# Half-width weight pieces, and the read-in product M of batch 0 made in two halves

## The chip, the cores and the metric

The kernel runs on one core of a Trainium2 chip. The time is the device time of one execution in microseconds (us). Times given with a profile come from one profiled execution; its span runs from the first to the last instruction of the program.

The engines are TensorE (PE; its weight loads are listed as PEld), VectorE (DVE), ScalarE (ACT), GpSimd (POOL) and SyncE (SP), whose queue issues the transfers (DMA). Each engine works through its own instructions in program order, and waits in that order for what the others deliver.

## The reference, cut to what matters

Attention between 512 tokens and 32 state rows per head goes both ways, and its result runs through an expert block, `w_in`, gelu, `w_out`.

```python
scores = scale * x @ state.T              # B=8, H=8, S=512, Ns=32, D=64
a = softmax(scores);  xread = a @ state
a2 = softmax(scale * state @ x.T);  sread = a2 @ x
y = concat([xread, sread], axis=2)        # (B,H,S+Ns,D) -> (B*(S+Ns), H*D) = (4352, 512)
h = y @ w_in                              # 512 -> 2048
out = (h * sigmoid(1.702 * h)) @ w_out    # 2048 -> 512
```

Both weights come as 64-bit floats and are used as 32-bit ones.

## The kernel before, in words

**The product M.** Since `xread` is `a @ state`, the up product of the token rows is `a @ (state @ w_in)`. For each batch b and each chunk c of 512 columns of `w_in` the kernel makes M(b, c) = state @ w_in[:, c] first, by heads (`att_M`, 16 matmul records of a 64x32 tile by 512 columns through `by_state`, L320, into two PSUM tiles, each copied to SBUF by ACT, L460). The up products then need two contractions over 128 instead of four: `up_x(b, f)` multiplies 128 columns of M by the normalised, transposed weights `aT` of the attention (L524, four records) and ACT applies the gelu (L527). The columns f = 4c to 4c + 3 belong to chunk c. `turn(b, c, then, n)` makes the four up products of a chunk, puts `att_M(*then)` ahead of the last of them, and rounds pieces of weights after the first ones.

**PSUM.** Two pools of two banks each serve this stage: `psA` (`att_ps`: transposes, M, and up products marked spare) and `psH` (up products, warming matmuls, and an M marked spare, such as M(1,0)). A bank is written again only after its last reader is done.

**The weights.** SP loads 64-bit words in 32 pieces of 512 KB (`PIECES`, `load_weight`, L185): 16 of `w_in`, chunk by chunk, each 128 rows by 512 columns, then 16 of `w_out`. Each is turned into 32-bit floats by DVE and ACT: `mask` (DVE, L207), two Relus on ACT for `w_in` (`round_a`, L218 and L219), then `fraction` (L225) and three steps of `round_b` (L236, L239, L243) on DVE. `powers_to(n)` runs the first part for the pieces up to n, `round_to(n)` the second, which also runs the first part three pieces ahead; `rounds(n)` does n more pieces. Program order is written out by hand, so the place of each such call in the list at the end of the kernel (from L1131 on) sets the order on DVE, ACT and SP.

**The start.** Two pieces are loaded, then state and x of batch 0, two more pieces, state and x of batch 1, the rest. `att_xT_arriving` transposes x of batch 0 as it lands and makes its scores in halves; `att_scores` makes the scores of the other direction. DVE subtracts the maxima, ACT takes the exponential (L1146), and `att_x_norm` (L403 to L408) normalises and transposes into `aT`. Batch 1 follows with `att_state`, `att_xT`, `att_scores`, `att_blocks` (L351), `att_x_exp` (L394 to L396) and `att_x_norm`; its `aT` lies in the tile `low`, beside the working rows of the pieces. `keep_warm(n)` fills PE with n matmuls on zeros (L125). M(0,0) is made whole, after piece 3 and after the scores of batch 1; up products 0 to 3 of batch 0 follow, M(1,0), piece 4 and `att_x_norm(1)`, and then turns of four between the two batches. From the first product with `w_out` on (L542, near 78 us), and for the later batches, nothing in the code differs.

Of the kernel before, what the change touches and what calls it, by code (L numbers as in the profile page):

```python
# [10 lines left out]
FP32 = mybir.dt.float32  # L11
I32 = mybir.dt.int32
U32 = mybir.dt.uint32
AF = mybir.ActivationFunctionType
# [6 lines left out]
def kernel(  # L21
# [30 lines left out]
    nc = tc.nc  # L52

    B, H, S, D = x.shape
# [27 lines left out]
    mpool = ctx.enter_context(tc.tile_pool(name="mpool", bufs=1))  # L82
# [4 lines left out]
    psH = ctx.enter_context(tc.tile_pool(name="psH", bufs=2, space=bass.MemoryType.PSUM))  # L87
# [4 lines left out]
    def att_ps(shape, name):  # L92
        return psA.tile(shape, FP32, tag="att", name=name)
# [16 lines left out]
    low = konst.tile([P, 6, S], FP32, name="low")  # L110
# [51 lines left out]
    w_in = [konst.tile([P, NPR, FC], FP32, name=f"w_in_{c}") for c in range(NFC)]  # L162
    w_out = konst.tile([P, NF, DM], FP32, name="w_out")
    w_in_words, w_out_words = moe_w_in.bitcast(I32), moe_w_out.bitcast(I32)

    PIECES = [("i", c, k) for c in range(NFC) for k in range(NPR)] + [("o", f) for f in range(NF)]
    raw, power, begun = {}, {}, {}
    AHEAD = 3

    def load_weight(i):  # L170

        key = PIECES[i]
        nin, room = NFC * NPR, NF // 2
        if i < room or nin - NPR <= i < nin:
            o = 2 * (i % room if i < room else i - (nin - NPR))
            raw[i] = w_out[:, o : o + 2].rearrange("p f n -> p (f n)").bitcast(I32)
        else:
            o = 2 * (i % 4)
            raw[i] = later[:, o : o + 2].rearrange("p f n -> p (f n)").bitcast(I32)
        if key[0] == "i":  # L180
            _, c, k = key
            src = w_in_words[P * k : P * (k + 1), 2 * FC * c : 2 * FC * (c + 1)]
        else:
            src = w_out_words[P * key[1] : P * (key[1] + 1)]
        nc.sync.dma_start(raw[i], src)  # L185

# [6 lines left out]
    for i, v in enumerate((8.0 * most, 8.0 * (most - least))):  # L193
        t = konst.tile([P, 1], FP32, name=f"edge_{i}")
        nc.gpsimd.memset(t, v)
        edge.append(t)

    def words(i):
        w = raw[i].rearrange("p (n w) -> p w n", w=2)
        return w[:, 0].bitcast(U32), w[:, 1]  # L200

    def mask(i):

        _, hi = words(i)
        sc = low[:, 2 + i % (AHEAD + 1)].bitcast(I32)
        power[i] = sc
        nc.vector.tensor_scalar(sc, hi, 0x7FF00000, None, ALU.bitwise_and)  # L207

    def round_a(i):

        if i not in power:
            mask(i)
        sc = power[i]
        if PIECES[i][0] == "o":
            nc.vector.tensor_scalar(sc, sc, most, least, ALU.min, ALU.max)
            nc.vector.tensor_scalar(sc, sc, -least, 8.0, ALU.add, ALU.mult)
            return
        nc.scalar.activation(out=sc.bitcast(FP32), in_=sc, func=AF.Relu, bias=edge[0], scale=-8.0)  # L218
        nc.scalar.activation(out=sc, in_=sc.bitcast(FP32), func=AF.Relu, bias=edge[1], scale=-1.0)  # L219

    def fraction(i):

        key = PIECES[i]
        dst = w_in[key[1]][:, key[2]] if key[0] == "i" else w_out[:, key[1]]
        nc.vector.tensor_scalar(dst.bitcast(I32), words(i)[1], 0xFFFFF, 0x100000, ALU.bitwise_and, ALU.bitwise_or)  # L225
        begun[i] = dst

# [87 lines left out]
    def by_state(b, ps, rhs):  # L315

        for j in range(NPR):
            for g in range(NG):
                rows, st = slice(D * g, D * (g + 1)), slice(Ns * j, Ns * (j + 1))
                nc.tensor.matmul(ps[g][st], A[b]["stT"][rows, st], rhs(rows, j), start=True, stop=True)  # L320
# [77 lines left out]
    def att_x_norm(b):  # L398

        a = A[b]  # L400
        t = a["e1"].rearrange("p g i n -> p (g i) n")
        sm = apool.tile([P, NS1], FP32, tag="sm", name=f"sm_{b}")
        nc.vector.reduce_sum(out=sm, in_=t, axis=AX.X)  # L403
# [4 lines left out]
        nc.vector.transpose(  # L408
            a["aT"].rearrange("p g t -> p (g t)"), a["e1"].rearrange("p g i n -> p (g i n)")
        )  # L410
# [37 lines left out]

    turns = {"M": 0}

    def att_M(b, c, spare=False):

        m = mpool.tile([P, NG, FC], FP32, tag=f"M{turns['M'] % NFC if b < 2 else c}", name=f"M_{b}_{c}")
        turns["M"] += 1
        A[b]["M", c] = m
        name = f"M_{b}_{c}_"
        ps = [psH.tile([P, FC], FP32, tag="h", name=name + str(g)) if spare else att_ps([P, FC], name + str(g)) for g in range(NG)]
        by_state(b, ps, lambda rows, j: w_in[c][rows, j])
        for g in range(NG):
            nc.scalar.copy(m[:, g], ps[g])  # L460


    squares = dram.tile([Ns, NG * NB, NPR, Ns], FP32, name="squares")
# [53 lines left out]

    G = {}

    def up(key, f, ntok, lhs, rhs, spare=False):  # L520
        hps = att_ps([P, ntok], f"h_{key}_{f}") if spare else psH.tile([P, ntok], FP32, tag="h", name=f"h_{key}_{f}")
        n = len(lhs)
        for i in range(n):
            nc.tensor.matmul(hps, lhs[i], rhs[i], start=(i == 0), stop=(i == n - 1))  # L524
        if f % 2 == 0:
            G[key, f // 2] = free.pop(0)
        nc.scalar.activation(out=G[key, f // 2][:, f % 2, :ntok], in_=hps, func=AF.Gelu_apprx_sigmoid)  # L527

    def up_x(b, f, spare=False):
        c, o = divmod(P * f, FC)  # L530
        m = A[b]["M", c]
        up(b, f, S, [m[:, g, o : o + P] for g in range(NG)], [A[b]["aT"][:, g] for g in range(NG)], spare)

    O = {}

# [589 lines left out]
    nper = FC // P  # L1125

    def rounds(n):
        round_to(done["b"] + n)
# [16 lines left out]
    powers_to(3)  # L1145
    nc.scalar.activation(out=A[0]["e1"], in_=A[0]["e1"], func=AF.Exp, scale=scale)  # L1146
    att_scores(0)
    powers_to(2)
    round_to(3, 0)
    powers_to(4)  # L1150
    att_x_norm(0)
    keep_warm(24)
    att_state(1)
    for j in range(NPR):
        keep_warm(2)
        att_xT(1, j)
    att_scores(1)
    keep_warm(3)
    powers_to(4)
    round_to(NPR, 1)  # L1160
    att_M(0, 0)
    powers_to(NPR + 2)


    att_blocks(1)
    att_x_exp(1)
    up_x(0, 0)
    up_x(0, 1)
    up_x(0, 2, True)
    up_x(0, 3, True)  # L1170

# [4 lines left out]
    def turn(b, c, then, n=()):  # L1176

        for i in range(nper):
            if i == nper - 1 and then:
                att_M(*then)  # L1180
            up_x(b, nper * c + i)
            if i < len(n):
                rounds(n[i])

    turn(1, 0, None, [1, 1, 1])
    att_M(0, 1)
    turn(0, 1, (1, 1), [1, 1, 1])
    round_to(3 * NPR)
    turn(1, 1, (0, 2), [1, 1])
    round_to(4 * NPR)  # L1190
# [77 lines left out]
    for b in range(1, B):  # L1268
# [23 lines left out]
        k = 3 if b + 1 < B else 0  # L1292
# [40 lines left out]
```

## Time and profile before

| | |
|---|---|
| median of 8 runs | 713.93 us (713.71 to 714.02) |
| profiled execution | 713.95 us |
| its span | 712.2 us |
| PE busy | 697.9 us |
| DVE busy | 602.1 us |
| ACT busy | 231.3 us |
| pieces of `w_in`: transfers | 16 of 512 KB |
| moved by DMA | 77.10 MB |

The table's busy times are sums over the span. The kernel has stages with different limits, so the views by stage, the timeline and the chain of waits (the work that ended last, followed back) say more than they do. In a timeline line stand the start and the duration in us, the engine, the line of the kernel, the operation, what it writes and reads with shape, how many instructions were merged, and in brackets how long the engine had been idle and what released it. In a line by stage each engine has its busy time and the number of its instructions.

### The profile page before, as it was taken

How to read it: one execution, taken by the hardware profiler on the slowest of the kernel's cores; microseconds unless marked ns; L12 is line 12 of the kernel's file. 1: busy time of each engine (PE TensorE's matmuls, PEld its weight loads, DVE VectorE, ACT ScalarE, POOL GpSimd, SP SyncE). 2: the span in 40 equal slices, each digit the busy share in tenths (PEclk: the TensorE clock that was granted, in tenths of full speed). 3: DMA queues.
4: the chain of work that ended last, by engine and by line, in shares of the span. 5: the costliest groups of instructions: out<-in, count | busy, mean ns of one | idle time of the engine just before them, and what ended most of it. 6: DMA issues, size and time to landing. Idle time of an engine off the chain costs nothing.

```text
span 712.2 us, 12665 instructions
## 1 busy us (share of the span) xinstructions
PE 697.9 (98%) x4975; PEld 557.8 (78%) x4975; DVE 602.1 (85%) x1246; ACT 231.3 (32%) x456; POOL 0.8 (0%) x8
## 2 busy tenths in 40 slices
PE   8989999999999999999999999999999999999996
PEld 3433444457888799888998899879987998899995
DVE  6999899979987999789968997899789997888650
ACT  5686511023214322433233322441343224300210
POOL 0000000000000000000000000000000000000000
PEclk9999999999999999999999999999999999999999
DMA  8921246217743194408550574138431940031001
GB/s 232 365 78 53 93 147 141 117 44 189 188 130 62 34 202 143 88 0 180 164 120 1 112 205 120 29 70 193 140 61 35 201 146 22 0 115 65 16 1 29
DMA packets 143770, 77.10 MB, mean 108 GB/s; under 512 B 113888, under 2 KB 127712, under 8 KB 143712
## 3 DMA queue, kind: packets, MB, share of 16 engines
q1 hardware_dynamic: 143712, 76.31, 41.4%
q8 instruction: 39, 0.64, 0.4%
q14 instruction: 19, 0.16, 0.1%
HBM read 60.29 MB, written 15.99 MB: 107 GB/s over the span
## 4 chain that ended last, share of the span: by engine, by line
PE 93%; ACT 2%; DVE 2%; DMA 2%; SPq 0%; issue 0%; DVEq 0%; ACTq 0%
PE low L696 21%; PE o L1058 17%; PE o L745 14%; PE o L696 10%; PE o L542 8%; PE h L524 7%; PE upx L1058 6%; PE M L320 4%; PE o L585 2%; PE o L320 1%; PE sr L500 1%; PE warm L125 1%; PE upx_sr L1058 1%; DMA out_dram<-osb_sr 1%; DMA xn<-in_x_dram 1%; DVE g L752 1%
## 5 line engine op out<-in xcount | busy, mean ns | idle before, releaser
L1068 DVE TENSOR_TENSOR g<-o,g 128x512 f32<-128x512 f32 (+1 forms) x140 | 88.0, 650 | 51.1 <-PE o L1058 50.1
L745 PE MATMUL o<-w_out,g 128*128 128x256 f32 x448 | 100.5, 380 | 0.0
L745 PEld LDWEIGHTS o<-w_out,g 128*128 128x128 f32 x448 | 84.2, 190 | 16.9 <-issue 5.5
L1065 ACT ACTIVATE g<-g 128x512 f32<-128x512 f32 (+1 forms) x84 | 49.8, 600 | 100.9 <-DVE g L1068 100.9
L1058 PE MATMUL upx<-aT,M 128*128 128x256 f32 x192 | 49.3, 379 | 0.0
L1058 PE MATMUL o<-ta,M 128*128 128x256 f32 x192 | 49.3, 379 | 0.0
L1058 PE MATMUL o<-ta,ms 128*128 128x256 f32 x192 | 48.3, 379 | 0.0
L696 PE MATMUL low<-low,g 128*128 128x128 f32 x336 | 44.4, 275 | 0.0
L460 ACT COPY M<-M 128x512 f32<-128x512 f32 x64 | 33.2, 596 | 28.1 <-PE M L320 28.1
L696 PEld LDWEIGHTS low<-low,g 128*128 128x128 f32 x336 | 40.9, 192 | 0.0
L1058 PEld LDWEIGHTS o<-ta,ms 128*128 128x128 f32 x192 | 36.5, 190 | 5.0
L1058 PEld LDWEIGHTS o<-ta,M 128*128 128x128 f32 x192 | 36.5, 190 | 5.0
L1058 PEld LDWEIGHTS upx<-aT,M 128*128 128x128 f32 x192 | 36.0, 190 | 4.6
L696 PE MATMUL low<-sums,later 128*128 128x128 f32 x280 | 37.1, 275 | 0.0
L696 PEld LDWEIGHTS low<-sums,later 128*128 128x128 f32 x280 | 34.6, 192 | 0.6 <-ACT pu L705 0.2
L320 PE MATMUL M<-w_in,stT 64*32 64x512 f32 x512 | 32.7, 594 | 0.2 <-ACT eT L490 0.2
L524 PE MATMUL h<-low,M 128*128 128x512 f32 x64 | 29.7, 600 | 1.5 <-DVE low L408 1.5
L696 PE MATMUL low<-w_out,g 128*128 128x128 f32 x224 | 29.7, 275 | 0.9 <-DVE pu L701 0.9
L524 PE MATMUL h<-aT,M 128*128 128x512 f32 x64 | 28.7, 599 | 1.4 <-ACT M L460 1.4
L542 PE MATMUL o<-w_out,g 128*128 128x512 f32 x64 | 28.7, 594 | 0.0
L542 PE MATMUL o<-w_out,sums 128*128 128x512 f32 x64 | 28.4, 594 | 0.0
L696 PEld LDWEIGHTS low<-w_out,g 128*128 128x128 f32 x224 | 27.3, 192 | 1.1 <-DVE pu L701 1.1
(208 smaller groups left out, 1282.5 us busy)
## 6 DMA issues: line engine op xcount, KB each, us to landing
low<-low SPq DMA_DIRECT2D x78, 256.0 KB, 3.9
later<-in_moe_w_out_dram SPq DMA_DIRECT2D x16, 512.0 KB, 3.4
xn<-in_x_dram SPq DMA_DIRECT2D x28, 256.0 KB, 4.7
low<-low SPq DMA_DIRECT2D x9, 768.0 KB, 5.3
w_out<-in_moe_w_in_dram SPq DMA_DIRECT2D x12, 512.0 KB
xsq<-in_x_dram SPq DMA_DIRECT2D x96, 64.0 KB, 2.3
out_dram<-osb SPq DMA_DIRECT2D x18, 256.0 KB, 3.2
out_dram<-later SPq DMA_DIRECT2D x14, 256.0 KB, 2.2
```

Of the source, the lines that this page charges most:

```text
L125: nc.tensor.matmul(ps, zeros[:, :P], zeros, start=True, stop=True)
L320: nc.tensor.matmul(ps[g][st], A[b]["stT"][rows, st], rhs(rows, j), start=True, stop=True)
L460: nc.scalar.copy(m[:, g], ps[g])
L500: nc.tensor.matmul(ps[st, g], a["eT"][:, g, c, st], xn[b][:, c, NG * j + g], start=(c == 0), stop=(c == SCH - 1),)
L524: nc.tensor.matmul(hps, lhs[i], rhs[i], start=(i == 0), stop=(i == n - 1))
L542: nc.tensor.matmul(ops, G[key, f // 2][:, f % 2, P * r : P * (r + 1)], w_out[:, f], start=(f == 0), stop=(f == NF - 1))
L585: nc.tensor.matmul(ps[:, r], lhs[f][:, P * r : P * (r + 1)], rhs[:, f], start=(first and r == 0 and f == 0), stop=(f == HF - 1), skip_grou ...
L696: nc.tensor.matmul(ps, lhs[f], rhs[:, f], start=(first and f == 0), stop=(f == QF - 1), skip_group_check=True)
L745: nc.tensor.matmul(ps[:, r], lhs[f][:, P * r : P * (r + 1)], rhs[:, f], start=(r == 0 and f == 0), stop=(f == HF - 1), skip_group_check=True,)
L1058: nc.tensor.matmul(ps[:, k], lhs[i][:, o : o + P], rhs[i], start=(first and k == 0 and i == 0), stop=(i == n - 1), skip_group_check=True,)
L1065: nc.scalar.activation(out=dst, in_=src, func=AF.Gelu_apprx_sigmoid)
L1068: nc.vector.tensor_tensor(out=dst, in0=ps, in1=x, op=ALU.add)
```

## The change

A piece of `w_in` becomes two blocks of 128 rows by 256 columns (in one transfer, with runs of 2 KB in place of 4 KB), in the order chunk, half of the columns, pair of row blocks. So the first two pieces of a chunk hold all rows of its first 256 columns. All steps of the conversion see a piece as 2 x 256.

`att_M` gets a parameter `h`: with 0 or 1 it makes one half of the columns of M, with half as many columns per matmul and per copy. M(0,0) and M(0,1) are made so. The first half of M(0,0) goes right after the scores of batch 0, and 18 warming matmuls follow in place of 24. Up products 0 and 1 of batch 0, which need this half alone, go ahead of the end of piece 3; their gelus are held in a list and issued by `gelus()` after the exponential of batch 1. The second half follows. The first half of M(0,1) goes into the first turn of batch 1, ahead of its last up product, and the second half after up product 4 of batch 0; the turn of batch 0 over chunk 1 is written out for this.

```diff
-    PIECES = [("i", c, k) for c in range(NFC) for k in range(NPR)] + [("o", f) for f in range(NF)]
+    PIECES = [("i", c, h, k) for c in range(NFC) for h in range(2) for k in range(2)] + [("o", f) for f in range(NF)]
...
         if key[0] == "i":
-            _, c, k = key
-            src = w_in_words[P * k : P * (k + 1), 2 * FC * c : 2 * FC * (c + 1)]
+            _, c, h, k = key
+            n0 = 2 * FC * c + FC * h
+            src = w_in_words[2 * P * k : 2 * P * (k + 1), n0 : n0 + FC].rearrange("(k p) n -> p k n", k=2)
+            nc.sync.dma_start(raw[i].rearrange("p (k n) -> p k n", k=2), src)
         else:
-            src = w_out_words[P * key[1] : P * (key[1] + 1)]
-        nc.sync.dma_start(raw[i], src)
+            nc.sync.dma_start(raw[i], w_out_words[P * key[1] : P * (key[1] + 1)])
...
+    def halved(t):
+        return t.rearrange("p (k n) -> p k n", k=2)
+
     def words(i):
-        w = raw[i].rearrange("p (n w) -> p w n", w=2)
+        w = raw[i].rearrange("p (k n w) -> p w k n", k=2, w=2)
         return w[:, 0].bitcast(U32), w[:, 1]
...
-        sc = low[:, 2 + i % (AHEAD + 1)].bitcast(I32)
+        sc = halved(low[:, 2 + i % (AHEAD + 1)]).bitcast(I32)
...
-        dst = w_in[key[1]][:, key[2]] if key[0] == "i" else w_out[:, key[1]]
+        if key[0] == "i":
+            _, c, h, k = key
+            dst = w_in[c][:, 2 * k : 2 * k + 2, FC // 2 * h : FC // 2 * (h + 1)]
+        else:
+            dst = halved(w_out[:, key[1]])
...
-    def att_M(b, c, spare=False):
+    def att_M(b, c, spare=False, h=None):
...
+        if not h:
+            A[b]["M", c] = mpool.tile([P, NG, FC], FP32, tag=f"M{turns['M'] % NFC if b < 2 else c}", name=f"M_{b}_{c}")
+            turns["M"] += 1
+        m = A[b]["M", c]
+        n0, n = (0, FC) if h is None else (FC // 2 * h, FC // 2)
...
+        by_state(b, ps, lambda rows, j: w_in[c][rows, j, n0 : n0 + n])
         for g in range(NG):
-            nc.scalar.copy(m[:, g], ps[g])
+            nc.scalar.copy(m[:, g, n0 : n0 + n], ps[g])
...
+    held = []
+
+    def gelus():
+        for out, hps in held:
+            nc.scalar.activation(out=out, in_=hps, func=AF.Gelu_apprx_sigmoid)
+        held.clear()
+
+    def up(key, f, ntok, lhs, rhs, spare=False, hold=False):
...
-        nc.scalar.activation(out=G[key, f // 2][:, f % 2, :ntok], in_=hps, func=AF.Gelu_apprx_sigmoid)
+        held.append((G[key, f // 2][:, f % 2, :ntok], hps))
+        if not hold:
+            gelus()
...
     att_scores(0)
+    att_M(0, 0, h=0)
     powers_to(2)
     round_to(3, 0)
     powers_to(4)
     att_x_norm(0)
-    keep_warm(24)
+    keep_warm(18)
...
     att_scores(1)
     keep_warm(3)
+
+    up_x(0, 0, hold=True)
+    up_x(0, 1, hold=True)
     powers_to(4)
     round_to(NPR, 1)
-    att_M(0, 0)
+    att_M(0, 0, h=1)
     powers_to(NPR + 2)
-
-
     att_blocks(1)
     att_x_exp(1)
-    up_x(0, 0)
-    up_x(0, 1)
+    gelus()
     up_x(0, 2, True)
     up_x(0, 3, True)
...
-    turn(1, 0, None, [1, 1, 1])
-    att_M(0, 1)
-    turn(0, 1, (1, 1), [1, 1, 1])
+    turn(1, 0, (0, 1, False, 0), [1, 1, 1])
+    up_x(0, nper)
+    rounds(1)
+    att_M(0, 1, h=1)
+    up_x(0, nper + 1)
+    rounds(1)
+    up_x(0, nper + 2)
+    rounds(1)
+    att_M(1, 1)
+    up_x(0, nper + 3)
```

More of the change, by code (lines that the diff above doesn't have):

```diff
@@ L449 @@
     turns = {"M": 0}
-    def att_M(b, c, spare=False):
[L453 to L458, printed above, removed]
+    def att_M(b, c, spare=False, h=None):
[4 more added lines that the diff above has]
+        n0, n = (0, FC) if h is None else (FC // 2 * h, FC // 2)
+        name = f"M_{b}_{c}_{h}_"
+        ps = [psH.tile([P, n], FP32, tag="h", name=name + str(g)) if spare else att_ps([P, n], name + str(g)) for g in range(NG)]
+        by_state(b, ps, lambda rows, j: w_in[c][rows, j, n0 : n0 + n])
         for g in range(NG):
-            nc.scalar.copy(m[:, g], ps[g])
+            nc.scalar.copy(m[:, g, n0 : n0 + n], ps[g])
     squares = dram.tile([Ns, NG * NB, NPR, Ns], FP32, name="squares")
@@ L518 @@
     G = {}
-    def up(key, f, ntok, lhs, rhs, spare=False):
+    held = []
[4 more added lines that the diff above has]
+    def up(key, f, ntok, lhs, rhs, spare=False, hold=False):
         hps = att_ps([P, ntok], f"h_{key}_{f}") if spare else psH.tile([P, ntok], FP32, tag="h", name=f"h_{key}_{f}")
@@ L526, in up, with up_x @@
             G[key, f // 2] = free.pop(0)
-        nc.scalar.activation(out=G[key, f // 2][:, f % 2, :ntok], in_=hps, func=AF.Gelu_apprx_sigmoid)
-    def up_x(b, f, spare=False):
+        held.append((G[key, f // 2][:, f % 2, :ntok], hps))
+        if not hold:
+            gelus()
+    def up_x(b, f, spare=False, hold=False):
         c, o = divmod(P * f, FC)
         m = A[b]["M", c]
-        up(b, f, S, [m[:, g, o : o + P] for g in range(NG)], [A[b]["aT"][:, g] for g in range(NG)], spare)
+        up(b, f, S, [m[:, g, o : o + P] for g in range(NG)], [A[b]["aT"][:, g] for g in range(NG)], spare, hold)
     O = {}
```

## The prediction

> **What bounds the kernel now.** I read the page first: sections 1 and 4, for which engine carries the end.
>
> ```profile
> span 712.2 us, 12665 instructions
> PE 697.9 (98%) x4975; PEld 557.8 (78%) x4975; DVE 602.1 (85%) x1246; ACT 231.3 (32%) x456; POOL 0.8 (0%) x8
> PE 93%; ACT 2%; DVE 2%; DMA 2%; SPq 0%; issue 0%; DVEq 0%; ACTq 0%
> ```
>
> TensorE (PE) is the bound; 14 us of the span are without a matmul, so the change, which touches only the first 55 us, can win only what PE loses there. Next the busy times by stage (PE, PEld, DVE, ACT, POOL; clock; DMA share; GB/s).
>
> ```profile
> 14.00:26.00 12.00, 12.00 (x84) 5.62 (x68) 11.70 (x21) 7.67 (x12) 0.00 (x0) 1.00 0.98 295
> 26.00:37.50 11.50, 9.36 (x49) 3.32 (x48) 11.29 (x18) 8.37 (x14) 0.00 (x0) 1.00 0.81 326
> 37.50:46.60 9.10, 8.39 (x32) 3.26 (x32) 9.10 (x19) 8.94 (x16) 0.00 (x0) 1.00 0.02 4
> 46.60:55.00 8.40, 8.38 (x33) 3.23 (x34) 8.40 (x18) 6.71 (x12) 0.00 (x0) 1.00 0.59 193
> ```
>
> PE idles 2.1 us in the second row and 0.7 in the third; VectorE (DVE) is full in all, ScalarE (ACT) in the third. The timeline names what ends PE's waits, and the chain of waits says through whom the third row runs.
>
> ```profile
> 30.03 1.06 ACT L396 ACTIVATE e<-e 128x1024 f32<-128x1024 f32 x1 [0.26 <-DVE e L395]
> 33.06 1.21 DVE L403 TENSOR_REDUCE sm<-e 128x32 f32<-128x1024 f32 x1
> 36.17 1.25 DVE L408 STREAM_TRANSPOSE low<-e 128x1024 f32<-128x1024 f32 x1
> 37.56 7.11 PE L524 MATMUL h<-low,M 128*128 128x512 f32 x16 [1.46 <-DVE low L408]
> 44.13 0.71 DVE L243 SCALAR_TENSOR_TENSOR w_in<-w_in,low 128x512 f32<-128x512 f32 x1
> 44.60 1.35 PE L320 MATMUL M<-w_in,stT 64*32 64x512 f32 x16
> 46.62 5.42 PE L524 MATMUL h<-aT,M 128*128 128x512 f32 x12 [0.67 <-ACT M L460]
> ```
>
> ```profile
> 35.09 1.13 PE M L320 x16
> 36.22 1.05 ACT M L460 x2
> 37.27 0.63 ACT low L218
> ...
> 45.57 0.48 ACT g L527
> 46.05 0.53 ACT M L460
> 46.58 0.04 issue
> 46.62 5.42 PE h L524 x12
> ```
>
> Two things fix the start of batch 1's first up product (37.56): its weights' transpose on DVE, ready at 37.42, and M(1,0). DVE has no idle entry from 14.06 to 74, so 37.42 is a sum of DVE work. From 36.22 to 46.58 the chain is ACT without a gap: copies of M(1,0), five pairs of Relu (L218, L219), four gelus, first copy of M(0,1). From 46.62 on PE runs without a wait to 82, and the chain is nearly all PE afterwards: a shift at 46 to 55 reaches the end.
>
> **What the Trainium skill says.** "VectorE: DVE Perf Modes", section "What auto-detection actually checks": a one-source operation in SBUF runs two elements per cycle if the outermost non-unit dimensions of source and destination are both even or equal. The trace agrees that such a mode is on: L225 (one source) 418 ns, L243 (two sources) 692, both 128x512. The new 2x256 destinations have an even outer count, so I keep 418. "ScalarE: Activation LUTs", "What ACT_TABLE_LOAD costs": a change of function set costs a load of about 1283 ns; the trace has 1.28 us at 31.11 between exponential and gelu. Holding the gelus avoids two more loads. "TensorE: Matmul & The Clock Gate", "What's actually happening": PE's clock halves after an idle window of about 3.4 us. The first 16 warming matmuls took 5.99 us, the later 24 took 5.29, which fits.
>
> **The change, part by part.** The sum is against the profiled execution: span 712.2, time 713.95, 1.75 around it; the median of the runs is 713.93.
>
> *Pieces.* The bytes, the number of transfers and of DVE and ACT instructions per piece stay. A row run becomes 2 KB in place of 4. In the trace's packet records a 2 KB packet takes 84 ns (median), a 4 KB one 159: per piece 16 x 84 = 1.34 us on each DMA engine against 8 x 159 = 1.27, so +0.07. Two pieces lie ahead of x of batch 0, whose first chunk is on the chain (DMA 3.05 to 8.34), and DVE's unbroken run hangs on it: +0.15 on everything. Bounds: 0, if the queue hides it, and +0.4, if SP's issue (0.40 us each, as for 128 runs) grows by half for each of two pieces. I take 0.15. Ahead of x of batch 1 it is four pieces, +0.3. Later pieces are loaded by about 27 and first needed after that; DVE hides them. No transfer changes its place on SP's queue.
>
> *M(0,0), first half, after the scores of batch 0.* PE 14.83 to about 15.35 (a full M takes 1.02 to 1.15; half of it). Six fewer warming matmuls take off 6 x 0.22 = 1.32. ACT makes two half copies after the exponential that ends at 17.6: 128x512 takes 0.59 and 128x128 0.24, so about 0.36 each, 0.31 in a row; ACT is idle there until 19.11, nothing waits. The state transpose of batch 1 moves from 20.1 to 19.4, but its copy on ACT still waits behind the Relus that end at 20.59, and batch 1's x may land only around 20. So its scores end at about 24.9, not 25.42.
>
> *Two up products ahead.* Three warming matmuls, then 2 x 1.72 = 3.44 (16 records in 6.87): 25.65 to 29.1. M(0,0) second half to 29.6. On ACT everything that stood behind the copies of M(0,0) moves with them: copies to 30.3 (before: 28.4), Relus of piece 5 to 31.65, exponential of batch 1 to 32.7 (before: 31.1). DVE wants it at 33.06, since the work on piece 4 stands ahead; the cover is 0.4 us, and every tenth beyond it would be a tenth on 37.42. Hence the early matmuls win nothing at 37.42.
>
> *Held gelus.* Table load to 34.0, the two held gelus to 35.1. They hold both banks that M(1,0) writes, so PE has it from 35.1 to 36.1, and ACT copies it from 36.2, after the gelus of products 2 and 3: the stall of PE before 37.56 is only divided anew. ACT's unbroken run starts at 37.2 as before at 37.27.
>
> *M(0,1) by halves.* Before, it waited for piece 7 (44.84) and for ACT. Now the first half, from pieces 4 and 5 (done by 39.9), goes to PE at about 42.9, ahead of product 3 of batch 1. On ACT its copies stand behind the Relus of piece 10, but ahead of the gelu of product 3: the first is out at about 45.9 (the old 46.58 less one gelu, 0.48, and 0.2 for the half size). Product 4 starts at 45.95 in place of 46.62: 0.67 won. Then the second half of M takes 0.52 on PE, which before was done by then: 0.15 left. The rest of the idle 0.5 comes back at M(1,1): its copies are ready at ACT's pace at about 54.4, and PE, which has no wait in between beyond 0.1, starts product 4 of batch 1 at about 54.5, before at 54.83. So 0.3 won, start delay included. Two more copy instructions (0.2) are in these ACT times; PE waits for none of them elsewhere.
>
> Sum: 712.2 - 0.3 = 711.9, plus 1.75 is **713.6 us**. A ceiling: after 37.56 PE loses 46.62 - 37.56 - 6.88 - 1.02 = 1.16 in all, and nothing takes work off DVE ahead of 37.42. More than 1.16 would need a cause I don't see.
>
> **The rivals.**
> 1. *ACT is not in the way*: the order leaves its copies earlier, and PE's loss of 1.16 goes but for the start delay: 712.9. For it: ACT idles 1.6 us before 48.64. Against: the unbroken ACT chain. 0.14.
> 2. *The exponential comes too late*: x of batch 1 lands late and the 0.4 us of cover is overdrawn, by 0.5 say; transpose and ACT's run shift with it: 714.4. For it: DMA is at 98% up to 26. 0.12.
> 3. *M(0,1)'s first half waits for piece 7 after all*, because its columns lie between those of pieces 6 and 7 and these are written earlier in program order. Then it runs at 44.84 to 45.35, product 3 behind it to 47.07, product 4 and the second half to 49.3; product 4 of batch 1 at about 55.6: +0.8, 714.7. 0.08.
> 4. *The other side, PE's clock.* From 33.3 to 37.5 PE would have one M of 1.0 us in small tiles and 3.2 us of idleness; before it had only 1.5 idle there. If that makes an idle window of 3.4 us, matmuls run at half speed for at least one more: 1.7 us of work lost, no more than 0.3 of it in waits: about 715.5, and 717 for two windows. Against: between 9.6 and 13.3 PE had as little and the matmuls after it took 0.22. It decides from about 3.4 us nearly empty on. 0.08.
> 5. *DVE loses its two-per-cycle mode on the halved shapes*: 9 one-source operations between 14 and 37.4, each 0.27 longer, 2.4 us on 37.42: about 716.5. Against: the skill's rule. 0.04.
>
> **How the numbers follow.** The likeliest case, 713.6, has 0.5 (its own range 713.1 to 714.1); the rivals 0.46; 0.04 is unnamed. No difference below 0.2%, 1.4 us, counts as one: that is about what a measurement of this kernel can tell from no change. The first three cases and most of the third rival lie inside it, which is 0.78 with some of it given to unknowns; slower (rivals 4 and 5, the tails of 2 and 3) 0.14; faster 0.08, since the ceiling is under the bound. The range 712.7 to 715.2 leaves out rivals 4 and 5 and the far ends.
>
> **What would show it.** Right: product h<-low,M still starts near 37.6, released by DVE; the exponential near 31.7; M L320 by halves near 15, 29 and 43; then a wait of PE of about 0.7 to 1.2 us before 46 for ACT's M copy; PE without waits from there. Wrong: L225 over 0.5 us (rival 5); h matmuls of 0.8 us or records at twice their spacing after 37 (rival 4); M at 44.8 (rival 3); L403 later than 33.3 and released by ACT (rival 2). The forecast fails as a whole if DVE's run before 37.42 gets longer or shorter, or if ACT's copies are out well before 45.5.

## The result and the profile after

The changed kernel takes 716.26 us (median of 11 runs, 715.21 to 717.06) beside 713.88 us for the kernel before (31 runs, 713.71 to 714.42). The ratio is 1.0033, with a 95% interval of 1.0025 to 1.0041: 2.4 us slower, outside the forecast range. The profiled execution took 716.06 us with a span of 714.3, so the 1.76 around the span are as before and the loss lies inside it. Two executions of 1,874 and 4,146 us, one of b_fetch_osb2 and one of b_pieces_osb2, are left out of all ratios below; the first is b_fetch_osb2's profiled one, so no profile of it is read.

Line numbers after 200 moved: products of the token rows are L542 (before L524), M is L329 (L320) with its copies at L471 (L460), gelu L535 (L527), the sums for batch 1 L412 (L403), its transpose L417 (L408), the copy of a finished row block of the output L569 (L549).

The page of the changed kernel, its span, the busy times and the shares of the chain that ended last:

```profile
span 714.3 us, 12724 instructions
...
PE 699.0 (98%) x5001; PEld 558.2 (78%) x5001; DVE 602.1 (84%) x1246; ACT 231.3 (32%) x460; POOL 0.8 (0%) x8
...
PE 87%; DVE 7%; DMA 3%; ACT 2%; issue 1%; SPq 0%; DVEq 0%; ACTq 0%
```

PE is busy 1.1 us more, DVE's and ACT's sums are the same. The chain is PE's for 87% of the span in place of 93%, DVE's for 7% in place of 2%: some 40 us of the chain are no longer PE's. The busy times by stage (PE, PEld, DVE, ACT, POOL; clock; DMA share; GB/s), in the two rows of the prediction that matter here:

```profile
26.00:37.50 11.50, 8.85 (x48) 3.00 (x46) 11.29 (x18) 7.63 (x13) 0.00 (x0) 0.98 0.89 330
37.50:46.60 9.10, 9.10 (x32) 3.58 (x32) 9.10 (x20) 8.04 (x14) 0.00 (x0) 0.84 0.01 4
```

The clock column, the share of its full clock that PE was granted, stood at 1.00 before; in the second of these rows it is 0.84 now. Cut finer, it says 0.98 in 36.5 to 37, 0.50 up to 40 and 0.61 in 40 to 40.5: half speed from 36.98 to 40.39, which is 3.41 us. The timeline (start, duration, idle time before and its releaser) and the chain of waits of the changed kernel over the same stretch:

```profile
34.51 1.57 PE L329 MATMUL M_None<-w_in,stT 64*32 64x512 f32 x16 [0.81 <-ACT g L535]
37.41 6.86 PE L542 MATMUL h<-low,M 128*128 128x512 f32 x12 [1.32 <-DVE low L417]
```

```profile
37.41 3.44 PE h L542 x4
40.86 0.02 issue
40.88 0.60 ACT g L535
...
46.54 0.27 ACT M L471
...
46.85 1.98 PE h L542 x4
```

The first up product of batch 1 starts at 37.41, released by DVE's transpose, as forecast; but it takes 3.44 us, and the forecast had 1.72. ACT idles until that product is done (40.88), and product 4 of batch 0 starts at 46.85, not at 45.95. From 60 to 154 us the instructions of DVE and ACT stand 0.96 us later than before.

That is less than half of the loss. At 160 us the distance to the kernel before jumps to 2.15 us and stays there to the end. The chain of waits of the changed kernel at that place:

```profile
152.28 2.02 DMA out_dram<-osb
154.41 0.59 ACT osb L569
155.02 3.24 DMA out_dram<-osb
158.36 0.59 ACT osb L569
...
162.21 0.70 DVE later L585
...
179.05 1.16 PE o L716 x8
```

This is the down product of the first rows (`down`), code that the change doesn't touch. ACT copies each row block of 128x512 into one buffer, `osb`, and SP sends it off; the next copy waits until the transfer has read that buffer. The first and the third transfer (at 158.97, left out here) take 2.02 us, the second takes 3.24. Behind the copies stand a gelu on ACT and then a run of DVE from 162.21 to 179.0, with PE at its end. Before, the chain here was PE's up to 173.6, and the third copy waited 2.18 us, about as the others did. The ACT timeline at the third copy, of the kernel before and of the changed one:

```profile
156.20 0.59 ACT L549 COPY osb<-o 128x512 f32<-128x512 f32 x1 [2.18 <-DMA out_dram<-osb]
158.36 0.59 ACT L569 COPY osb<-o 128x512 f32<-128x512 f32 x1 [3.37 <-DMA out_dram<-osb]
```

What is different at 155 us? The packet records of the trace have a queue of instruction fetches (the page: 39 packets of the kind "instruction" on q8, before and after; 0.64 MB in all, 16 KB each). Set against PE's instructions, one comes after some 256 of them in the mean (160 to 320 in the kernel before). One packet falls at 160.5 us before (0.95 us long) and at 155.9 us after (1.21 us long), both times after some 1,440 PE instructions. The change adds 26 pairs of matmul and weight load ahead of that point: 16 for each M made by halves, less six warming matmuls. That is 52 instructions, a fifth of the distance between two fetches, and it moves the packet into the second transfer.

The packet records also show what it does there. The transfer has 128 packets of 2 KB. Of these, 120 are over at 156.68; the other eight begin at 157.08, just when the fetch ends (155.87 + 1.21), and the last ends at 157.77. Eight of 128 is a sixteenth, and the page counts 16 DMA engines for the core: the fetch held up the share of one of them, though the records don't name the engine. In the kernel before, the same thing happens to the fourth transfer (120 packets over at 161.21, eight from 161.41 on), and no copy waits behind that one. This delay of one output transfer, with the copy that waits for it, is called the collision below.

### The profile page after: what moved, and what is told of

Its sections match the earlier page's. It is cut to its first block, busy times and chain, and to the rows that moved or that the text cites. A ratio compares the mean times of both kernels' runs of the same rounds, so it can differ in the third digit from the quotient of the medians.

```text
span 714.3 us, 12724 instructions
## 1 busy us (share of the span) xinstructions
PE 699.0 (98%) x5001; PEld 558.2 (78%) x5001; DVE 602.1 (84%) x1246; ACT 231.3 (32%) x460; POOL 0.8 (0%) x8
## 4 chain that ended last, share of the span: by engine, by line
PE 87%; DVE 7%; DMA 3%; ACT 2%; issue 1%; SPq 0%; DVEq 0%; ACTq 0%
PE low L716 20%; PE o L1078 17%; PE o L765 12%; PE o L716 10%; PE o L562 7%; PE h L542 6%; PE upx L1078 6%; PE M_None L329 3%; PE o L605 2%; PE sr L511 1%; DMA out_dram<-osb 1%; PE upx_sr L1078 1%; DMA out_dram<-osb_sr 1%; DVE g L772 1%; PE o L329 1%; DMA xn<-in_x_dram 1%
## 5 line engine op out<-in xcount | busy, mean ns | idle before, releaser
L1078 PEld LDWEIGHTS o<-ta,M 128*128 128x128 f32 x192 | 36.5, 190 | 5.0
L1078 PEld LDWEIGHTS o<-ta,ms 128*128 128x128 f32 x192 | 36.5, 190 | 5.0
L471 ACT COPY M<-M_None 128x512 f32<-128x512 f32 x60 | 31.1, 597 | 25.4 <-PE M_None L329 25.4
L716 PE MATMUL low<-sums,later 128*128 128x128 f32 x280 | 37.1, 275 | 1.2 <-ACT pu L725 1.2
L542 PE MATMUL h<-low,M 128*128 128x512 f32 x64 | 31.4, 625 | 1.3 <-DVE low L417 1.3
L329 PE MATMUL M_None<-w_in,stT 64*32 64x512 f32 x480 | 30.7, 594 | 1.0 <-ACT g L535 0.8
L542 PE MATMUL h<-aT,M 128*128 128x512 f32 x64 | 29.2, 601 | 0.6 <-ACT M L471 0.5
```

What stands on the lines that cost most here:

```text
L471: nc.scalar.copy(m[:, g, n0 : n0 + n], ps[g])
L716: nc.tensor.matmul(ps, lhs[f], rhs[:, f], start=(first and f == 0), stop=(f == QF - 1), skip_group_check=True)
L1078: nc.tensor.matmul(ps[:, k], lhs[i][:, o : o + P], rhs[i], start=(first and k == 0 and i == 0), stop=(i == n - 1), skip_group_check=True,)
```

## The experiments

Three theories. **F (fetch)**: the moved fetch delays the second output transfer, and this costs 1.2 us in the profile, perhaps more in the median. **H (half clock)**: the stretch from 33.7 to 37.4, in which PE has only the small-tile M(1,0), makes its clock fall to half. **D (the order)**: the early part of the change is at fault by itself, by its pieces, by M(0,1) in halves, or by the place of the exponential. All experiments start from one of the two kernels.

**b_fetch**: the kernel before with 26 more pairs of PE instructions, and nothing else. The warming keeps its length.

```diff
...
-    keep_warm(24)
+    keep_warm(50, 246)
```

The helper's new second argument is the width of a matmul, 512 columns where it is left out; the lines that add it are not shown.

> The kernel before, with its 24 warming matmuls of 512 columns near 15 us made 50 of 246 columns: the same work on PE, 26 more pairs of weight load and matmul, as many as the change adds. Theory F (PE's instruction fetch of 16 KB meets the second transfer of an output row block, which ACT waits for): the fetch at 160.5 us moves to about 155, the wait of ACT's third osb copy grows from 2.2 to about 3.4 us, the time is 1.1 us longer, 715.0. Rival (that transfer is late because of the half pieces or of the later PE): no change, 713.9, the wait stays at 2.2.

715.9 us (13 runs, ratio 1.0029 [1.0021, 1.0037]; expected 715.0). Not an instruction of the change is in it, and it loses 2.0 us. The fetch packet is at 155.0. Its ACT timeline at the third copy:

```profile
157.54 0.59 ACT L549 COPY osb<-o 128x512 f32<-128x512 f32 x1 [3.57 <-DMA out_dram<-osb]
```

The wait for the second transfer is 3.57 us in place of 2.18. DVE's run behind it moves from 0.05 us earlier than before to 1.35 later: 1.40 us for the collision. In its packet records eight packets of the second transfer begin at 156.14, where the fetch ends (155.02 + 1.12). F stands; the median moved by more than the profiled execution (715.25).

**a_fetch**: the other way round, the changed kernel with 18 more pairs.

```diff
...
-    keep_warm(18)
+    keep_warm(36, 256)
```

> The changed kernel, with its 18 warming matmuls of 512 columns made 36 of 256: 18 more pairs on PE, no other work. Theory F: the fetch at 155.9 us moves ahead of the output transfers, to about 149, the wait of the third osb copy is 2.2 us again, and the time is 1.1 us shorter than the changed kernel, about 715.1; the stretch near 37 to 40 us at half clock stays. Rival: no change from 716.3.

713.8 us (13 runs, 1.0003 [0.9995, 1.0011]). The fetch is at 144.4, the second transfer is on time, and the whole loss of the median is gone, where only 1.1 us had been expected to go (715.1). The profiled execution also had no half clock in this stage (1.00 from 4.3 us to 710), which shows that it isn't in every execution. Three of the 13 have a granted clock of 0.995 and take 714.75, 715.33 and 715.67; the other ten lie between 713.65 and 714.31. Its PE timeline, the measure for the parts of the change without the two troubles:

```profile
42.46 0.66 PE L329 MATMUL M<-w_in,stT 64*32 64x256 f32 x16
...
45.58 1.98 PE L542 MATMUL h<-aT,M 128*128 128x512 f32 x4 [0.55 <-ACT M L471]
47.50 0.66 PE L329 MATMUL M<-w_in,stT 64*32 64x256 f32 x16
48.09 3.77 PE L542 MATMUL h<-aT,M 128*128 128x512 f32 x8
51.79 1.09 PE L329 MATMUL M_None<-w_in,stT 64*32 64x512 f32 x16
...
54.63 2.74 PE L542 MATMUL h<-low,M 128*128 128x512 f32 x6
```

**b_pieces**: the kernel before with the half-width pieces, M whole.

```diff
-    PIECES = [("i", c, k) for c in range(NFC) for k in range(NPR)] + [("o", f) for f in range(NF)]
+    PIECES = [("i", c, h, k) for c in range(NFC) for h in range(2) for k in range(2)] + [("o", f) for f in range(NF)]
...
```

> The kernel before with the half-width pieces alone (two row blocks by 256 columns, all steps on 2 x 256, all M whole and at their old places). The prediction's step: x of batch 0 comes 0.15 us later and so does everything, 714.05. The rival, read off the profile of the changed kernel: DVE starts 0.5 us and PE's first transposes 0.2 us earlier, so 0.2 us shorter, 713.7. L225 stays near 0.42 us in either.

713.59 us (13 runs, 0.9998 [0.9990, 1.0006]), 0.34 under its kernel before; in the profile the stage stands 0.35 us earlier. In its DVE timeline the first mask starts at 4.43 in place of 4.95 and PE's first transpose of x at 7.95 in place of 8.39: the start doesn't get later, it gets earlier. So D does not hold for the pieces. Its PE timeline against that of a_fetch:

```profile
46.27 5.42 PE L532 MATMUL h<-aT,M 128*128 128x512 f32 x12 [0.69 <-ACT M L468]
51.62 1.09 PE L328 MATMUL M<-w_in,stT 64*32 64x512 f32 x16
...
54.48 2.84 PE L532 MATMUL h<-low,M 128*128 128x512 f32 x6
```

With the halves, product 4 of batch 0 starts at 45.58 in place of 46.27, 0.69 earlier. But from there to the start of M(1,1) PE takes 51.79 - 45.58 = 6.21 us in place of 51.62 - 46.27 = 5.35: the second half is 0.59 of the 0.86 (47.50 to 48.09), and 0.27 is lost around it. Product 4 of batch 1 starts at 54.63, with M whole at 54.48.

**a_m01whole**: a_fetch with M(0,1) whole in its old place, all else as changed.

```diff
-    turn(1, 0, (0, 1, False, 0), [1, 1, 1])
-    up_x(0, nper)
...
-    att_M(1, 1)
-    up_x(0, nper + 3)
+    turn(1, 0, None, [1, 1, 1])
+    att_M(0, 1)
+    turn(0, 1, (1, 1), [1, 1, 1])
```

> a_fetch with M(0,1) made whole at its old place; M(0,0) by halves, early products and held gelus stay. The prediction's step (the halves of M(0,1) win about 0.4 us): 714.2, so 0.4 slower than a_fetch. The rival, read off the profile of a_fetch (the halves start product 4 of batch 0 0.7 us earlier, and give it back as 0.6 for the second half and two waits of 0.26 for a second half copy): 713.6, 0.1 to 0.2 faster than a_fetch.

715.77 us (6 runs, 1.0032 [1.0021, 1.0044]), which looks as if the halves were worth 2 us. They aren't: with 16 pairs fewer the fetch is back at 154.8 and the third copy late again (it waits 3.94 us). Read ahead of that, from 60 to 154 us, it stands 0.22 us earlier than the kernel before, a_fetch 0.30: the halves of M(0,1) are worth 0.08 us. An edit made to isolate one part had put the other cause back.

**a_fetch_warm**: a_fetch with five warming matmuls right behind M(1,0).

```diff
     att_M(1, 0, True)
+    keep_warm(5, pool=psA)
```

> a_fetch with five warming matmuls on zeros between M(1,0) and the first up product of batch 1, in a bank of psA, in the 1.3 us in which PE waits for DVE. Theory C (PE stood nearly empty from 33.7 to 37.4 us and ran at half clock until 40.3): granted clock 1.00 from 37 to 41 us, the first up product of batch 1 takes 1.72 us in place of 3.44, about 1.1 us shorter than a_fetch, near 714.0 or a little below the kernel before. Rival (ACT's order and the half copies set the pace at 46 us, whatever the clock): clock 1.00, but product 4 of batch 0 still starts near 46.8 and the time stays within 0.3 us of a_fetch.

713.84 us (13 runs, 1.0002 [0.9994, 1.0010]); the lowest granted clock is 0.997, where a_fetch had 0.995 three times. The median is not lower, as the theory's 1.1 us would have it: most executions of a_fetch had no half clock to lose. Three executions of 714.94 to 715.12 remain, at clocks of 0.998 and 0.999: they have another cause, which no profile caught.

**c_early** and **c_early2** test D for the order on DVE and ACT: the rounding of piece 4 goes behind the normalisation of batch 1, so that 37.4 comes earlier; M(0,0)'s second half goes between products 0 and 1; c_early2 also runs the Relus two pieces ahead in place of three. The edit of c_early against a_fetch:

```diff
     up_x(0, 0, hold=True)
-    up_x(0, 1, hold=True)
     powers_to(4)
     round_to(NPR, 1)
     att_M(0, 0, h=1)
     powers_to(NPR + 2)
+    up_x(0, 1, hold=True)
...
     att_M(1, 0, True)
-    round_to(NPR + 1)
+    fraction(NPR)
     att_x_norm(1)
+    round_to(NPR + 1)
```

> a_fetch with piece 4's rounding moved behind the normalisation of batch 1 (only its first step stays ahead), and the second half of M(0,0) between up products 0 and 1, so that the exponential comes at 30 us. Theory D (DVE's order ahead of 37.4 us is what the early products lacked): aT of batch 1 is ready 1.5 to 1.9 us earlier, its first up product starts near 35.5, product 4 of batch 0 near 44.1 in place of 45.6; 712.4. Rival (piece 7, now later, or ACT takes it back): within 0.3 of a_fetch, 713.8.

> c_early with the Relus run two pieces ahead in place of three from piece 4 to 7, so that one pair of Relus (1.37 us) leaves ACT's queue ahead of the half copies of M(0,1). If ACT's queue sets the start of product 4 of batch 0: about 1 us earlier than c_early, 711.6. If DVE's piece 7 or the second half of M(0,1) does: as c_early, 712.4.

c_early: 713.8 us (13 runs, 0.9999 [0.9991, 1.0007]), where D had 712.4. Two lines of its PE timeline tell it:

```profile
35.30 3.67 PE L542 MATMUL h<-low,M 128*128 128x512 f32 x8 [1.00 <-DVE low L417]
45.68 1.98 PE L542 MATMUL h<-aT,M 128*128 128x512 f32 x4 [1.71 <-ACT M L471]
```

Batch 1 begins 1.8 us earlier than in a_fetch, and product 4 of batch 0 at 45.68 in place of 45.58. DVE owes the rounding that was put off, ACT's Relus wait for DVE's mask (the last pair ahead of the copies starts at 43.89), and the copies of M(0,1)'s half stand behind these Relus. The early start becomes a longer wait. c_early2: 715.77 us (10 runs, 1.0027 [1.0018, 1.0037]), where 711.6 or 712.4 had been expected; product 4 is at 45.38, but product 6 now waits 1.17 us for ACT, until 51.04, and five of its ten executions have a granted clock of 0.995 or 0.996. The profiled one (714.92) has no half clock in this stage, so the wait is most of its loss; where the others lose the rest isn't shown. Neither of these two orders makes this stage shorter.

**a_osb2**: the changed kernel with two output buffers in `down`, used in turn. The fetch stays where it is.

```diff
-            osb = opool.tile([P, DM], FP32, tag="osb", name=f"osb_{key}_{r}")
+            osb = opool.tile([P, DM], FP32, tag="osb" if r % 2 else "osd", name=f"osb_{key}_{r}")
```

> The changed kernel with two buffers for the four output row blocks of batch 0 (tags osd and osb in turn), instruction count and places unchanged. Theory F (the fetch holds up one output transfer, and that matters only because ACT's next osb copy waits for the buffer, with a gelu behind it): the fetch still stands at about 156 us, the copy doesn't wait, 1.2 to 2 us shorter than the changed kernel, 714.3 (713.7 to 715.4, the clock near 37 us still open). Rival (PE itself lacks instructions while the fetch runs): stays at 716.

712.9 us (21 runs, 0.9988 [0.9981, 0.9994]): 3.4 us below the changed kernel and 1.0 below the kernel before. The expected 714.3 (713.7 to 715.4) was too high; b_osb2 below shows why. The profiled execution had the half clock (0.996 in the mean, 713.97 us); three executions of 21 had 0.996 and took 713.97 to 714.25, the other 18 took 712.77 to 713.40. Against the median of 712.9 that is 1.1 to 1.4 us for the half clock.

**b_osb2**, **b_fetch_osb2**, **b_pieces_osb2**: the same buffer edit in the kernel before, in b_fetch and in b_pieces.

> The kernel before with two output buffers used in turn. Theory F (the copy of an output row block waits only for the transfer that frees its one buffer): in the kernel before that wait is short and lies beside PE's work, so the second buffer takes away the three waits of 2.2 us each but no more than about 0.3 us of the time: 713.6 to 713.9. Rival (the single buffer holds PE up in every batch, and the 0.98 us that the changed kernel with two buffers has over the kernel before is all from there): 712.9 or less.

> The kernel before with 26 more pairs of PE instructions in the warming (as in b_fetch, which took 715.9), and two output buffers. Theory F: PE's instruction fetch falls into the second output transfer again, near 155 us, but no copy waits for that transfer any more: within 0.3 us of the kernel before with two buffers and the old warming. Rival (the fetch holds PE itself up, or the 26 added pairs cost 2 us by themselves): 2 us above it, as 715.9 is above 713.9.

> The kernel before with the half-width pieces and two output buffers, M whole. If the pieces' 0.35 us earlier start and what the buffers give add up: 0.3 to 0.4 below the kernel before with two buffers. Against the changed kernel with two buffers (712.9): the theory that the halves of M, the held gelus and the two products ahead give nothing has it level or lower, 712.5 to 713.0; the rival that they give the 0.7 us that product 4 of batch 0 starts earlier has it at 713.4 or more.

b_osb2 takes 713.07 us (21 runs, 0.9987 [0.9981, 0.9994]). F's number for it, 713.6 to 713.9, was wrong: the second buffer is worth 0.85 us even without a collision. The ACT timeline of b_osb2, third and fourth copy:

```profile
153.39 0.58 ACT L549 COPY osb<-o 128x512 f32<-128x512 f32 x1 [1.30 <-DMA out_dram<-osb]
154.29 0.58 ACT L549 COPY osb<-o 128x512 f32<-128x512 f32 x1 [0.32 <-DMA out_dram<-osb]
```

The fourth copy starts at 154.29 in place of 158.94. DVE's run behind it begins 3.78 us earlier, but only 1.0 us is left by 178 us, because PE then takes the end over: in b_osb2 the chain from 150 to 182 us is PE alone. So in the kernel before, this place was 1 us beyond PE already, and whatever was added to the copies reached the end.

b_fetch_osb2 takes 713.14 us (0.9990 [0.9983, 0.9996]), 0.07 above b_osb2, where the same 26 pairs cost 2.0 us with one buffer. This settles F: the added instructions and the fetch cost no more than 0.07 us by themselves; the loss is the copy that waits for a buffer. b_pieces_osb2 takes 712.87 us (0.9985 [0.9978, 0.9991]), 0.2 below b_osb2 (0.3 to 0.4 had been expected) and level with the 712.9 of a_osb2, which has the whole change. With the collision out of the way the kernels are: before 713.07, with the pieces 712.87, with pieces and everything else 712.9. The pieces are worth 0.2 us; the halves of M, the early products and the held gelus nothing that these medians show.

The runs that decide on F, side by side (the fetch and the copy's wait from the profiled execution, all in us):

| kernel | output buffers | fetch at | third copy waits | median |
|---|---|---|---|---|
| before | 1 | 160.5 | 2.18 | 713.88 |
| changed | 1 | 155.9 | 3.37 | 716.26 |
| b_fetch | 1 | 155.0 | 3.57 | 715.9 |
| a_fetch | 1 | 144.4 | 2.16 | 713.8 |
| a_m01whole | 1 | 154.8 | 3.94 | 715.77 |
| b_osb2 | 2 | 160.5 | 1.30 | 713.07 |
| a_osb2 | 2 | 155.9 | 1.30 | 712.9 |
| b_fetch_osb2 | 2 | not read | not read | 713.14 |

**a_osb2_warm**: a_osb2 with the five warming matmuls of a_fetch_warm.

> The changed kernel with two output buffers and five warming matmuls in the idle time of PE after M(1,0) (10 more pairs with their weight loads at most). Theory of the clock (the stretch from 33.3 to 37.4 us, with 1.6 us of small-tile matmuls in it, halves PE's clock in a part of the executions, for 1.0 to 1.3 us): no execution shows the half clock after 37 us, the median stays at 712.8 to 712.9 and the executions near 714 (3 of 21 without the warming) are gone. Rival (those come from elsewhere, or the clock halves in spite of the warming): the same share of them stays.

713.43 us (13 runs, 0.9995 [0.9987, 1.0004]): the median is 0.5 higher, not the same, and the theory's number is missed. The spans say why. Eleven of the 13 spans are 711.2 or 711.3 us, those with the half clock in a_osb2 were 712.2 to 712.5; the other two, 711.7 and 712.4, have clocks of 1.000 and 0.999, and no execution here is under 0.997. Taken with the pair a_fetch and a_fetch_warm, a half clock (a mean of 0.996 or less) is in 6 of 34 executions without the warming matmuls and in 0 of 26 with them. Chance alone would do that about 3 times in 100, so H is well supported, not proved. But in six executions the time around the span is 2.64 to 3.29 us in place of 1.75. The packet records have one more PE fetch, at 713.4 us, 2.2 us behind the last instruction of the span; a_osb2, with ten PE instructions fewer, hasn't got it. That the end of the execution waits for this fetch fits both numbers, and wasn't tried further. The PE timeline where the warming sits:

```profile
35.97 1.25 PE L125 MATMUL warm<-sums 128*128 128x512 bf16 x4
37.31 4.96 PE L542 MATMUL h<-low,M 128*128 128x512 f32 x11
```

**a_again** and **a_warm**: the changed kernel once more, and with the five warming matmuls, to divide its loss between F and H.

> The changed kernel once more, beside the next one on the same chip. If two causes add (the output copy behind PE's instruction fetch in every execution, the half clock in some), its times spread over more than 1 us with a median near 716.2, and an execution without the half clock lies near 715.3 to 715.8, as those of b_fetch do.

> The changed kernel with five warming matmuls after M(1,0), as in a_osb2_warm, and the one output buffer it has. The 10 added PE instructions move the fetch by a tenth of a microsecond or two, so it still falls into the second output transfer. If the half clock after 37 us is in most executions of the changed kernel (share near 0.7 or more): the median falls by 0.7 to 1.2 against the changed kernel beside it. If it is in a part of them only, as with two buffers (3 of 21): by 0.4 at most, and the whole rest of the loss is the collision. If the last fetch of PE comes after the end, as it did in a_osb2_warm, up to 1.5 us lie around the span in some executions: the spans are to be compared.

a_again: 715.51 us (7 runs, 715.09 to 716.83, 1.0030 [1.0018, 1.0041]; expected was a median near 716.2). Its profiled execution (715.09) had no half clock: 0.28 us earlier than before from 74 to 154 us, 1.14 later from 160 on. The collision alone makes it slower, by 1.42 us at that place. a_warm: 716.21 us (5 runs, 1.0040 [1.0026, 1.0053]), no lower. Its profile shows no half clock at 37, but one at another place (columns as above):

```profile
175.00:176.00 1.00, 0.00 (x0) 0.00 (x0) 0.96 (x3) 0.99 (x3) 0.00 (x0) 1.00 0.00 0
177.00:178.00 1.00, 1.00 (x7) 1.00 (x7) 1.00 (x2) 0.57 (x1) 0.00 (x0) 0.56 0.18 27
```

The collision makes DVE late, PE idles 1.8 us between 174.8 and 176.6 (busy 0.79 in the slice before the first of these and 0.39 in the one between them), and from 177.1 to 180.5 the clock is at half. This execution started 1.3 us late too (the second piece landed late), and three of the five times have 2.35 to 2.71 around the span, as in a_osb2_warm; so its median can't divide F from H. It shows that a half clock in an execution of the changed kernel can come from the idle time behind the collision. b_fetch points the same way: it has nothing of the change, and 3 of its 13 executions, at 716.91 to 717.03, have a granted clock of 0.995 or 0.996, which none of the 41 executions of the kernel before beside it has.

The two profiled executions of the changed kernel, the one in the result and that of a_again, also suggest why the half clock comes in a part of the executions only. In both, PE has nothing but M(1,0) between 33.7 and 37.1. The trace's records of the clock, but for the last one, are multiples of 3.413 us long, and they begin elsewhere in each execution. In the result's, full clock lasts from 6.26 to 36.98, nine times 3.413; in a_again it begins at 6.83, and steps of 3.413 from there have edges at 34.14 and 37.55. So one such window of the first execution lies almost wholly in the empty stretch, and none of a_again does. The window before the fall, the same microseconds in a_again, and a_again's own window (columns as above):

```profile
33.57:36.98 3.41, 1.71 (x17) 0.31 (x16) 3.27 (x5) 3.16 (x7) 0.00 (x0) 1.00 0.64 239
33.57:36.98 3.41, 1.57 (x16) 0.31 (x16) 3.27 (x6) 3.16 (x8) 0.00 (x0) 1.00 0.46 169
34.14:37.55 3.41, 1.98 (x17) 0.61 (x18) 3.34 (x5) 3.17 (x7) 0.00 (x0) 1.00 0.28 103
```

## Why the prediction was wrong

**The loss.** In the profiled execution the span is 2.1 us longer. By the shifts: the start and the order of the stage -0.28 (a_again, which has no half clock at 37), the half clock 0.96 + 0.28 = 1.24, the collision 2.15 - 0.96 = 1.19. The sum is 2.15. In the medians the collision is the larger part: moving the fetch alone takes 716.26 to 713.8. How often the half clock adds to it isn't settled, since it comes in a part of the executions and in two places.

**The step that failed** is in "What bounds the kernel now" and in the sum: "the chain is nearly all PE afterwards: a shift at 46 to 55 reaches the end", and with it "the change, which touches only the first 55 us, can win only what PE loses there". The sum put everything behind 55 us at nothing. The runs show 1.19 us there in the profiled execution, 1.42 in a_again, at the output copies of 155 to 160 us: 26 more pairs of PE instructions move the fetch, so a change of instruction counts reaches further than its own stage. The page of before listed the instruction queue, and the trace showed ACT waiting three times 2.2 us for the one output buffer, with DVE's run and then PE behind it; I used neither, because the share of the chain said PE. No rival had this cause. "More than 1.16 would need a cause I don't see" was a ceiling on the gain; for the loss the prediction had none, and the chance of slower, 0.14, was too low for that.

**Rival 4**, the clock, with a chance of 0.08, came true in the profiled execution and in part of the others. Its price was "1.7 us of work lost": the first product took 3.44, 1.72 more; 1.24 of it reached the later stages. The point of decision, "about 3.4 us nearly empty", was too far out: in the 3.41 us before the clock fell at 36.98, PE was busy for 1.71 us, nearly all of it with its small-tile M(1,0) (1.57, forecast 1.0), and in those before 177.1 in a_warm it was idle for 1.8 only. A window half empty can be enough. It isn't always: in a_m01whole PE was busy 1.66 us in the window from 171.98 to 175.40, beside 1.59 in that of a_warm, and the clock stayed full, so where the limit lies stays open. The counter-argument, that PE "had as little" between 9.6 and 13.3, was a wrong reading: in the kernel before PE is busy 2.31 of these 3.7 us. The Trainium skill ("TensorE: Matmul & The Clock Gate", "What's actually happening") says that the clock halves after an idle window of about 3.4 us and that these windows are free-running. The length agrees (3.41), and so do the edges, which lie elsewhere in each execution (36.98 in the changed kernel's first, 37.55 in a_again); that the window has to be idle doesn't.

**Pieces**: the sign was wrong. The forecast was +0.15, from the packets' median time; measured were -0.34 (b_pieces) and -0.20 (b_pieces_osb2 against b_osb2). The first data land 0.5 us earlier, where the sum of packet times said later. Why the first landing comes earlier wasn't measured.

**M(0,0), first half; two products ahead; held gelus**: as forecast, except for the clock. The exponential starts at 31.51 (forecast 31.65), L412 at 32.90 (33.06 before), batch 1's first product at 37.41, by DVE. Rival 2 (late exponential) and rival 5 (DVE's mode: L234 still takes 0.42 us) are refuted by these lines. Rival 3 too: the first half of M(0,1) runs at 42.46 in a_fetch, not at 44.8. But dividing PE's stall, which I counted as free, made room for the half clock: before, products ran up to 35.0 and M(1,0) followed at once; now the products end at 33.7, and PE has only M(1,0) up to 37.4.

**M(0,1) by halves**: product 4 of batch 0 came 0.69 earlier in a_fetch than in b_pieces (forecast 0.67), the second half took 0.59 (0.52). "The rest of the idle 0.5 comes back at M(1,1)" failed: the second half and what is lost around it cost 0.86, more than the 0.69 won. Product 4 of batch 1 comes at 54.63, 0.2 earlier than before (forecast 0.3), but with the pieces alone it comes at 54.48. Against a_m01whole the halves bring 0.08 us.

Without the two troubles the change comes near its forecast, a_fetch 713.8 beside 713.6, but that is luck. The pieces were to cost 0.15 us and gained 0.35 in the profiled execution (b_pieces); everything else was to win 0.45 and lost 0.05 (0.30 earlier than before in a_fetch, 0.35 in b_pieces).

## What to carry to other kernels

A change early in a program that adds or takes away PE instructions moves the later instruction fetches, here from 160.5 to 155.9 us. Where a copy waits for the transfer out of its single buffer, look whether such a packet can fall into that transfer, and add a second buffer before tuning elsewhere: here one tag was worth 0.85 us in the kernel before and 3.4 in the changed one. When an experiment is to isolate one part, keep the number of PE instructions equal, or check in its profile that the far stages stand where they stood; otherwise it measures the shift. Ahead of a stall of PE that can't be removed, keep the work near it: here moving products away left PE busy for 1.71 of 3.41 us, and in a part of the executions its clock halved.

## What was not expected of the hardware

An instruction fetch of PE, one 16 KB packet of 0.9 to 1.5 us for some 256 PE instructions, lengthened a 256 KB output transfer from 2.02 to 3.24 us when it fell into it. Only a sixteenth of the transfer, eight packets of 128, waited for it, and they began when it ended (157.08 in the changed kernel, 156.14 in b_fetch). A fetch that comes behind the last instruction went with times that are 0.9 to 1.5 us longer around the span. The half clock came after 3.4 us with 1.57 us of matmuls in 64x32 tiles, and after 3.4 us with an idle gap of 1.8, in a part of the executions only; in each of the three profiled executions that have it, it lasted 3.4 us.
